# Mish as one ScalarE activation in the second feed-forward layer of a chunked attention kernel

## The chip, the cores and the metric

One NeuronCore of one Trainium2 chip. The metric is the device time of one execution in microseconds (us). Engines are named as in the profile: PE is TensorE, PEld its weight loads, DVE VectorE, ACT ScalarE, POOL GpSimd, SP SyncE, which issues the DMAs.

## What is computed

Attention within chunks of 64 tokens, then two feed-forward layers of width 512 to 2048 to 512 over 2304 tokens. The weights come as float64, the rest as float32. Of the reference, what matters:

```python
# attention per head, per chunk of 64 tokens: softmax(q k^T / sqrt(64)) v; x is its output, [2304, 512]
h = x @ moe_w_in;  r = np.maximum(h, 0.0);  g = s * (r * r) + b;  x = g @ moe_w_out      # layer one
h = x @ moe2_w_in                                                                       # layer two
sp = np.where(h > 20.0, h, np.log1p(np.exp(np.minimum(h, 20.0))))
g = h * np.tanh(sp)
out = g @ moe2_w_out
```

The last activation, h * tanh(softplus(h)), is what is called Mish.

## The kernel before

**Tiling.** Everything is held transposed on chip in `xT` (4 x 128 features by 2304 tokens). Each layer runs over five blocks of tokens; in layer one they have 512, 256, 512, 512 and 512 tokens, in layer two 512, 512, 512, 512 and 256. Per block a loop runs over 16 chunks `f` of 128 columns of d_ff. One step of it is `mm_in` (line 321: 12 matmuls into the PSUM tile `hp`), the activation (`ew1` or `ew2`) and `mm_out` of an earlier chunk (line 379: 12 matmuls into four accumulators). Each factor is split in a rounded part `hi` and a rest `lo`, and three products are taken (hi hi, lo hi, hi lo), which makes 24 matmuls of a full chunk. In the last block of layer two, with 256 tokens, a chunk has 12 matmuls of 256 columns and 6 of 512. `mm_out` comes one chunk behind `mm_in` in layer one, two behind in layer two (`LAG`), eight in the last block (`LASTLAG`).

**Activations.** `ew1` of layer one: ScalarE Relu out of PSUM (line 339), VectorE square and scale (340), ScalarE add (343), ScalarE Copy to `ghi` (344), GpSimd subtraction to `glo` (345). `ew2` of layer two computes tanh(log1p(e)) as m / (m + 2) with m = e (e + 2): VectorE minimum (355), ScalarE Exp (356), VectorE (357), ScalarE Ln (358), VectorE product with `hp` (359), ScalarE Exp (360), VectorE (362), GpSimd product (363), VectorE (364); then ScalarE Copy to `ghi` (367) and GpSimd subtraction to `glo` (368).

**Weights.** Each layer has 32 half-chunks (16 of `w_in`, 16 of `w_out`), loaded as pairs of 32-bit words (`wraw`) into room `w0_f` or `w1_f`, and made into float32 there. `decode_a`: ScalarE Abs of the upper words into the buffer `wdec` (line 105; three such buffers), VectorE clamp (106), shift (109), sign from `wraw` (113), bits of the lower words (117). `decode_b`: ScalarE Copy to `hi` (126), GpSimd subtraction to `lo` (127). Layer two's weights take the room of layer one's: in layer one's last block `w_in` of chunk f is loaded after the last use of layer one's, `w_out` one step later, and a decode comes in program order two steps after its load, at most two per step. By that, 27 of the 32 stand within layer one's last block, 5 at the start of layer two.

**Order.** The start, up to the first block, is written out by hand (`START`), the attention of the later tokens runs between steps of layer one (`at_stage`). Elsewhere the planner sets the order of instructions on each engine from a simulated timeline of its own, following program order where it can; each engine then runs its queue in that order. ScalarE's table set is chosen once ahead (line 399, `natural_log_exp_and_others`).

Of the kernel before, what the change touches and what calls it, by code (L numbers as in the profile page):

```python
# [8 lines left out]
F32 = mybir.dt.float32  # L9
F32R = mybir.dt.float32r  # L10
U32 = mybir.dt.uint32
AF = mybir.ActivationFunctionType
ALU = mybir.AluOpType
AX = mybir.AxisListType

P = 128
CH = 64
TB = 512
# [5 lines left out]
    "e2 t0 n2 t1 S3 X0 m3 T2 e3 X1 n3* A0 x0* w4 t2 T3 x1* t3 X2 A1 x2 B0 X3 w2 x3 h3 h0 h1 w5 w2 l0 l1* "  # L24
    "h2 l3* B1 l2"
)
# Upper words of float64 whose exponents are the ends of float32's range, read as float32.
UPPER_MIN = 2.0 ** -15
UPPER_MAX = (2.0 - 2.0 ** -3 - 2.0 ** -23) * 2.0 ** 16

# [2 lines left out]
def chunk_attention_moe_moe_kernel(  # L33
# [10 lines left out]
    w_out2: bass.AP,  # L44
    out: bass.AP,
):
    """The weights come as the 8-byte words of float64."""
    nc = tc.nc
    B, H, S, D = q.shape
    NT, DM = out.shape  # L50
# [4 lines left out]
    scale = 1.0 / float(D) ** 0.5  # L55
# [4 lines left out]
        1: [(sum(sizes1[:i]), n) for i, n in enumerate(sizes1)],  # L60
        2: [(sum(sizes2[:i]), n) for i, n in enumerate(sizes2)],
    }
    # 32-bit words: [..., column, (lower, upper)]
    w_dram = {
        1: (w_in1.bitcast(U32), w_out1.bitcast(U32)),
        2: (w_in2.bitcast(U32), w_out2.bitcast(U32)),
# [2 lines left out]
    sb = ctx.enter_context(tc.tile_pool(name="sb", bufs=1))  # L69
# [4 lines left out]
    ident = sb.tile([P, P], F32, name="ident")  # L74
    s_sb = sb.tile([P, 1], F32, name="s_sb")
    b_sb = sb.tile([P, 1], F32, name="b_sb")
    two = sb.tile([P, 1], F32, name="two")
    xT = sb.tile([P, KD, NT], F32, name="xT")

# [1 line left out]
    raw = {}  # L81
    wt = {}

# [16 lines left out]
    def decode_a(l, f, part):  # L100
        t = raw[l, f, part]
        a = sb.tile([P, DM], F32, tag="dec", bufs=NDEC, name="wdec")
        raw[l, f, part] = a
        u = a.bitcast(U32)
        nc.scalar.activation(out=a, in_=t[:, :, 1].bitcast(F32), func=AF.Abs)
        nc.vector.tensor_scalar(  # L106
            out=a, in0=a, scalar1=UPPER_MIN, scalar2=UPPER_MAX, op0=ALU.max, op1=ALU.min
        )
        nc.vector.tensor_scalar(  # L109
            out=u, in0=u, scalar1=3, scalar2=0x3FFFFFFF,  # L110
            op0=ALU.logical_shift_left, op1=ALU.bitwise_and,
        )
        nc.vector.scalar_tensor_tensor(  # L113
            out=u, in0=t[:, :, 1], scalar=0xC0000000, in1=u,
            op0=ALU.bitwise_and, op1=ALU.bitwise_or,
        )
        nc.vector.scalar_tensor_tensor(  # L117
            out=u, in0=t[:, :, 0], scalar=29, in1=u,
            op0=ALU.logical_shift_right, op1=ALU.bitwise_or,
        )  # L120
# [6 lines left out]
        nc.gpsimd.tensor_tensor(out=lo, in0=a, in1=hi.bitcast(F32), op=ALU.subtract)  # L127
        wt[l, f, part] = (hi, lo)

# [1 line left out]
    def runs(t0, n):  # L131
        done = 0
        while done < n:
# [2 lines left out]
            yield done, step, bb, ss  # L136
            done += step

    NS = 4  # tiles before the first block
    at = {}  # L140
    kbd = {}
    early = {}
# [10 lines left out]
        return ps_t.tile(shape, F32, tag="t", name="pt_")  # L153

    def sb_at(i, tag):
        """Tiles ahead of the first block use the room of weights that come later."""
        if i >= NS:
            if tag == "pt":  # in place of what was transposed
                return at[i]["e"].rearrange("p h s -> p (h s)")
            return atp.tile([P, DM], F32, tag=tag, name=tag)  # L160
        if (i, tag) not in early:
            pair = {"q": "w0_%d" % (15 - i), "k": "w0_%d" % (15 - i), "v": "w1_%d" % (15 - i),
                    "qt": "w1_%d" % (15 - i), "e": "w0_%d" % (11 - i), "pt": "w0_%d" % (11 - i)}
            two_t = sb.tile([P, 2, DM], F32, tag=pair[tag], name=tag)
            both = [x for x in pair if pair[x] == pair[tag]]
            for n, x in enumerate(both):
                early[i, x] = two_t[:, n]
        return early[i, tag]
# [107 lines left out]
            load_v(i + 1)  # L276

    def stages():
        """Softmax of a tile runs beside the transposes of the next one's operands."""
        yield [(NS, k_pe, k_out)]  # L280
        yield [(NS, q_pe, q_out)]
        for i in range(NS, NTILE):
            g = [(i - 1, x_pe, x_out)] if i > NS else []
            g.append((i, s_pe, s_max, s_exp, s_sum))
            if i + 1 < NTILE:
                yield g + [(i + 1, k_pe, k_out)]
                yield [(i + 1, q_pe, q_out)]
            else:
                yield g
            yield [(i, p_pe, p_out)]  # L290
        yield [(NTILE - 1, x_pe, x_out)]

# [1 line left out]
    def split_hi(t0, n, a):  # L294
        hi = sb.tile([P, TB], F32R, tag=f"xhi{a}", name=f"xhi{a}")[:, :n]
        nc.scalar.activation(out=hi, in_=xT[:, a, t0:t0 + n], func=AF.Copy)
# [28 lines left out]
        return hp  # L325

    def g_tiles(n, slot):
        if slot is not None:  # room of a weight chunk that has been used up
            t = sb.tile([P, 2, TB], F32R, tag=slot, name="g")
            return t[:, 0, :n], t[:, 1, :n]  # L330
        return (
            sb.tile([P, TB], F32R, tag="ghi", bufs=3, name="ghi")[:, :n],
            sb.tile([P, TB], F32R, tag="glo", bufs=3, name="glo")[:, :n],
        )
# [11 lines left out]
        return hi, lo  # L346

    def ew2(hp, n, slot):
        # tanh(log1p(e)) = m / (m + 2) with m = e * (e + 2)
        e = m2.tile([P, TB], F32, tag="e", bufs=2, name="me")[:, :n]  # L350
        m = m2.tile([P, TB], F32, tag="m", bufs=2, name="mm")[:, :n]
        hm = m2.tile([P, TB], F32, tag="hm", bufs=2, name="mh")[:, :n]
        r = m2.tile([P, TB], F32, tag="r", bufs=2, name="mr")[:, :n]
        hi, lo = g_tiles(n, slot)
        nc.vector.tensor_scalar(out=e, in0=hp, scalar1=20.0, scalar2=None, op0=ALU.min)
        nc.scalar.activation(out=e, in_=e, func=AF.Exp)  # L356
        nc.vector.scalar_tensor_tensor(out=m, in0=e, scalar=2.0, in1=e, op0=ALU.add, op1=ALU.mult)  # L357
        nc.scalar.activation(out=r, in_=m, func=AF.Ln, bias=two[:, 0:1])  # L358
        nc.vector.tensor_tensor(out=hm, in0=m, in1=hp, op=ALU.mult)  # L359
        nc.scalar.activation(out=r, in_=r, func=AF.Exp, scale=-1.0)  # L360
        # one Newton step on r = 1 / (m + 2)
        nc.vector.scalar_tensor_tensor(out=m, in0=m, scalar=2.0, in1=r, op0=ALU.add, op1=ALU.mult)  # L362
        nc.gpsimd.tensor_tensor(out=hm, in0=hm, in1=r, op=ALU.mult)  # L363
        nc.vector.scalar_tensor_tensor(  # L364
            out=hm, in0=m, scalar=2.0, in1=hm, op0=ALU.subtract, op1=ALU.mult, reverse0=True
        )
        nc.scalar.activation(out=hi, in_=hm, func=AF.Copy)  # L367
        nc.gpsimd.tensor_tensor(out=lo, in0=hm, in1=hi.bitcast(F32), op=ALU.subtract)  # L368
        return hi, lo

    def mm_out(l, f, g, acc, n):
# [24 lines left out]
    if True:  # L396
        atx = ExitStack()
        atp = atx.enter_context(tc.tile_pool(name="atp", bufs=1))
        nc.scalar.preload_act_table_set("natural_log_exp_and_others")
        order = sorted([(f, p) for f in range(NF) for p in range(2)], key=lambda z: (z[0] + z[1], z[1]))  # L400
        for w in LOADS.split():
            i = int(w[1:])
# [9 lines left out]
        with tc.manual_schedule():  # L412
            zero = sb.tile([P, P], F32, name="zero")
            nc.vector.memset(zero, 0.0)
            make_identity(nc, ident)
            nc.vector.memset(two, 2.0)
            warm = ps_t.tile([P, TB], F32, tag="t", name="warm")

            def warm_up(n):
# [53 lines left out]
        for si, (l, bi, f) in enumerate(steps):  # L473
            t0, n = blocks[l][bi]
            if (l, bi, f) == (2, 0, 0):
                atx.close()
                m2 = ctx.enter_context(tc.tile_pool(name="m2", bufs=1, reuse_waits="tile"))
# [3 lines left out]
            hp = mm_in(l, f, x, n)  # L481
# [50 lines left out]
```

## Time and profile before

| | us |
|---|---|
| median of 3 runs | 977.28 |
| lowest and highest | 977.11, 979.4 |
| span of the profiled execution, first to last instruction | 975.8 |

| stretch of the profiled execution | us |
|---|---|
| attention's first tiles and layer one up to its last block | 0 to about 435 |
| layer one, last block, with the decode of layer two's weights | about 435 to 550 |
| layer two, five blocks | about 550 to 972 |
| last evacuations and stores | to 975.8 |

The page gives the span alone; what an execution takes outside of it is in the times. Borders of blocks are blurred by some instructions of neighbouring blocks. Busy times overlap between engines, so they don't add up to the span; where an engine's idle time is listed, the instruction or engine that ended it stands behind the arrow.

### The profile page before, as it was taken

What the parts mean: (1) busy time and instruction counts of PE and PEld (TensorE: products, weight loads), DVE (VectorE), ACT (ScalarE), POOL (GpSimd) and SP (SyncE); (2) the same over time, 40 slices, a digit from 0 to 9 for tenths busy, and PEclk for the clock granted to TensorE, in tenths of its full rate; (3) what the DMA queues carried; (4) which work ended last, traced back from release to release, by engine and by line L of the source; (5) the groups of instructions that cost most, each with busy time, mean ns of one, the idle gap of its engine ahead of it and who ended that gap; (6) DMA issues with size and microseconds to landing.
All of it is one profiled execution on the core that took longest, in us unless ns stands there. A gap on an engine that the chain in (4) does not pass through costs nothing.

```text
span 975.8 us, 13100 instructions
## 1 busy us (share of the span) xinstructions
PE 901.6 (92%) x4880; PEld 732.4 (75%) x4880; DVE 645.9 (66%) x901; ACT 488.9 (50%) x852; POOL 437.8 (45%) x322
## 2 busy tenths in 40 slices
PE   8788779999999999999787788999999999999998
PEld 7656557998888888887565566887877787788786
DVE  5999994334222421138999998687668667866796
ACT  4655656555444533345555544454444445544553
POOL 3565553121122122225665457545554555555564
PEclk9999889999999999999899989999999999999999
DMA  8893101122211000016344100001001000100010
GB/s 186 265 346 99 33 23 44 44 55 45 47 40 33 15 9 1 1 44 193 108 151 134 60 1 1 1 6 38 1 1 44 1 1 1 44 1 0 1 45 21
DMA packets 81535, 53.27 MB, mean 55 GB/s; under 512 B 58688, under 2 KB 75072, under 8 KB 81472
## 3 DMA queue, kind: packets, MB, share of 16 engines
q1 hardware_dynamic: 81472, 52.44, 18.6%
q8 instruction: 38, 0.62, 0.3%
q14 instruction: 25, 0.20, 0.1%
HBM read 47.71 MB, written 4.72 MB: 54 GB/s over the span
## 4 chain that ended last, share of the span: by engine, by line
PE 35%; DVE 30%; ACT 10%; issue 9%; POOL 9%; SPq 3%; DMA 2%; POOLq 0%; ACTq 0%; DVEq 0%
PE acc L379 16%; PE hp L321 15%; POOL mh L363 7%; DVE wdec L113 5%; DVE mm L357 4%; DVE mh L364 4%; DVE wdec L117 4%; DVE wdec L106 4%; ACT ghi L367 3%; ACT mr L358 2%; DVE wdec L109 2%; ACT mr L360 2%; DVE mm L362 2%; DVE r L340 2%; DVE xlo L301 1%
## 5 line engine op out<-in xcount | busy, mean ns | idle before, releaser
L321 PE MATMUL hp<-xhi,w 128*128 128x512 f32 (+1 forms) x1280 | 377.0, 374 | 20.2 <-DVE mh L359 7.8
L321 PEld LDWEIGHTS hp<-xhi,w 128*128 128x128 f32 x1280 | 233.1, 190 | 66.9 <-DVE mh L359 10.1
L321 PE MATMUL hp<-xlo,w 128*128 128x512 f32 (+1 forms) x640 | 237.1, 372 | 4.2 <-DVE xlo L301 4.0
L345 POOL TENSOR_TENSOR glo<-r,ghi 128x512 fp32r<-128x512 f32 (+1 forms) x80 | 104.9, 1312 | 246.2 <-ACT ghi L344 202.8
L379 PE MATMUL acc<-ghi,w 128*128 128x512 f32 (+1 forms) x640 | 158.4, 388 | 16.1 <-ACT ghi L344 15.0
L340 DVE SCALAR_TENSOR_TENSOR r<-r,s_sb 128x512 f32<-128x512 f32 (+1 forms) x80 | 63.9, 800 | 164.3 <-ACT r L339 164.1
L363 POOL TENSOR_TENSOR mh<-mh,mr 128x512 f32<-128x512 f32 (+1 forms) x80 | 123.6, 1547 | 79.9 <-ACT mr L360 62.2
L379 PEld LDWEIGHTS acc<-ghi,w 128*128 128x128 f32 x640 | 114.4, 195 | 43.3 <-ACT ghi L344 19.2
L379 PE MATMUL acc<-w,ghi 128*128 128x512 f32 x516 | 134.6, 400 | 11.9 <-ACT ghi L367 11.2
L321 PEld LDWEIGHTS hp<-xlo,w 128*128 128x128 f32 x640 | 121.4, 190 | 26.7 <-DVE xlo L301 6.5
L127 POOL TENSOR_TENSOR w<-wdec,w 128x512 fp32r<-128x512 f32 x64 | 96.3, 1511 | 87.8 <-ACT w L126 83.6
L368 POOL TENSOR_TENSOR glo<-mh,ghi 128x512 fp32r<-128x512 f32 (+1 forms) x65 | 88.6, 1366 | 93.2 <-ACT ghi L367 93.2
L379 PEld LDWEIGHTS acc<-w,ghi 128*128 128x128 f32 x516 | 95.5, 190 | 41.6 <-ACT ghi L367 21.7
L367 ACT ACTIVATE ghi<-mh 128x512 fp32r<-128x512 f32 (+1 forms) x65 | 40.8, 628 | 96.7 <-DVE mh L364 96.6
L357 DVE SCALAR_TENSOR_TENSOR mm<-me 128x512 f32<-128x512 f32 (+1 forms) x80 | 76.5, 958 | 18.6 <-ACT me L356 18.4
L358 ACT ACTIVATE mr<-mm,two 128x512 f32<-128x512 f32 (+1 forms) x80 | 54.3, 681 | 68.2 <-DVE mm L357 67.9
L379 PE MATMUL acc<-glo,w 128*128 128x512 f32 (+1 forms) x320 | 83.4, 381 | 3.8 <-POOL glo L345 3.8
L364 DVE SCALAR_TENSOR_TENSOR mh<-mm,mh 128x512 f32<-128x512 f32 (+1 forms) x80 | 58.8, 737 | 41.9 <-POOL mh L363 41.6
L339 ACT ACTIVATE r<-hp 128x512 f32<-128x512 f32 (+1 forms) x80 | 43.8, 548 | 82.3 <-PE hp L321 81.2
L362 DVE SCALAR_TENSOR_TENSOR mm<-mm,mr 128x512 f32<-128x512 f32 (+1 forms) x80 | 59.1, 740 | 37.6 <-ACT mr L360 36.9
L126 ACT ACTIVATE w<-wdec 128x512 fp32r<-128x512 f32 x64 | 40.3, 630 | 79.1 <-DVE wdec L117 79.1
L343 ACT ACTIVATE r<-r,b_sb 128x512 f32<-128x512 f32 (+1 forms) x80 | 54.4, 680 | 38.8 <-DVE r L340 38.7
(301 smaller groups left out, 1101.9 us busy)
## 6 DMA issues: line engine op xcount, KB each, us to landing
wraw<-in_moe_w_out_dram SPq DMA_DIRECT2D x32, 512.0 KB, 4.4
wraw<-in_moe_w_in_dram SPq DMA_DIRECT2D x32, 512.0 KB, 4.8
v<-in_v_dram SPq DMA_DIRECT2D x72, 64.0 KB, 2.8
out_dram<-o SPq DMA_DIRECT2D x18, 256.0 KB, 2.2
k<-in_k_dram SPq DMA_DIRECT2D x16, 256.0 KB, 3.1
q<-in_q_dram SPq DMA_DIRECT2D x12, 256.0 KB, 3.0
k<-in_q_dram SPq DMA_DIRECT2D x4, 256.0 KB, 4.7
k<-in_k_dram SPq DMA_DIRECT2D x4, 128.0 KB, 5.8
```

What stands on the lines that cost most here:

```text
L127: nc.gpsimd.tensor_tensor(out=lo, in0=a, in1=hi.bitcast(F32), op=ALU.subtract)
L321: nc.tensor.matmul(out=hp, lhsT=w[:, sl], rhs=r, start=(a == 0 and p == 0), stop=(a == KD - 1 and p == 2),)
L340: nc.vector.scalar_tensor_tensor(out=r, in0=r, scalar=s_sb[:, 0:1], in1=r, op0=ALU.mult, op1=ALU.mult)
L345: nc.gpsimd.tensor_tensor(out=lo, in0=r, in1=hi.bitcast(F32), op=ALU.subtract)
L357: nc.vector.scalar_tensor_tensor(out=m, in0=e, scalar=2.0, in1=e, op0=ALU.add, op1=ALU.mult)
L358: nc.scalar.activation(out=r, in_=m, func=AF.Ln, bias=two[:, 0:1])
L362: nc.vector.scalar_tensor_tensor(out=m, in0=m, scalar=2.0, in1=r, op0=ALU.add, op1=ALU.mult)
L363: nc.gpsimd.tensor_tensor(out=hm, in0=hm, in1=r, op=ALU.mult)
L364: nc.vector.scalar_tensor_tensor(out=hm, in0=m, scalar=2.0, in1=hm, op0=ALU.subtract, op1=ALU.mult, reverse0=True)
L367: nc.scalar.activation(out=hi, in_=hm, func=AF.Copy)
L368: nc.gpsimd.tensor_tensor(out=lo, in0=hm, in1=hi.bitcast(F32), op=ALU.subtract)
L379: nc.tensor.matmul(out=acc[m][:, :n] if l == 1 else acc[m], lhsT=w[wi][:, sl] if l == 1 else g[gi][:, sl], rhs=g[gi] if l == 1 else w[wi], ...
```

## The change

`ew2` becomes three instructions: one ScalarE activation Mish out of PSUM into `r` (three buffers in place of two), the Copy to `ghi` and the subtraction to `glo`. In `decode_a` the Abs of layer two's weights (`l == 2`) becomes an and with 0x7FFFFFFF on VectorE; layer one's stay on ScalarE. The table set chosen ahead is `exp_and_others`, and the constant `two` goes.

```diff
-        nc.scalar.activation(out=a, in_=t[:, :, 1].bitcast(F32), func=AF.Abs)
+        if l == 1:
+            nc.scalar.activation(out=a, in_=t[:, :, 1].bitcast(F32), func=AF.Abs)
+        else:
+            nc.vector.tensor_scalar(
+                out=u, in0=t[:, :, 1], scalar1=0x7FFFFFFF, scalar2=None, op0=ALU.bitwise_and
+            )
...
     def ew2(hp, n, slot):
-        # tanh(log1p(e)) = m / (m + 2) with m = e * (e + 2)
-        e = m2.tile([P, TB], F32, tag="e", bufs=2, name="me")[:, :n]
-        m = m2.tile([P, TB], F32, tag="m", bufs=2, name="mm")[:, :n]
-        hm = m2.tile([P, TB], F32, tag="hm", bufs=2, name="mh")[:, :n]
-        r = m2.tile([P, TB], F32, tag="r", bufs=2, name="mr")[:, :n]
+
+        r = m2.tile([P, TB], F32, tag="r", bufs=3, name="mr")[:, :n]
         hi, lo = g_tiles(n, slot)
-        nc.vector.tensor_scalar(out=e, in0=hp, scalar1=20.0, scalar2=None, op0=ALU.min)
-        nc.scalar.activation(out=e, in_=e, func=AF.Exp)
-        nc.vector.scalar_tensor_tensor(out=m, in0=e, scalar=2.0, in1=e, op0=ALU.add, op1=ALU.mult)
-        nc.scalar.activation(out=r, in_=m, func=AF.Ln, bias=two[:, 0:1])
-        nc.vector.tensor_tensor(out=hm, in0=m, in1=hp, op=ALU.mult)
-        nc.scalar.activation(out=r, in_=r, func=AF.Exp, scale=-1.0)
-        # one Newton step on r = 1 / (m + 2)
-        nc.vector.scalar_tensor_tensor(out=m, in0=m, scalar=2.0, in1=r, op0=ALU.add, op1=ALU.mult)
-        nc.gpsimd.tensor_tensor(out=hm, in0=hm, in1=r, op=ALU.mult)
-        nc.vector.scalar_tensor_tensor(
-            out=hm, in0=m, scalar=2.0, in1=hm, op0=ALU.subtract, op1=ALU.mult, reverse0=True
-        )
-        nc.scalar.activation(out=hi, in_=hm, func=AF.Copy)
-        nc.gpsimd.tensor_tensor(out=lo, in0=hm, in1=hi.bitcast(F32), op=ALU.subtract)
+        nc.scalar.activation(out=r, in_=hp, func=AF.Mish)
+        nc.scalar.activation(out=hi, in_=r, func=AF.Copy)
+        nc.gpsimd.tensor_tensor(out=lo, in0=r, in1=hi.bitcast(F32), op=ALU.subtract)
         return hi, lo
...
-        nc.scalar.preload_act_table_set("natural_log_exp_and_others")
+        nc.scalar.preload_act_table_set("exp_and_others")
```

## Rows read from the trace of the kernel before

**Rows 1.** The page, part 1: span; busy time and share of TensorE and VectorE.
```profile
span 975.8 us, 13100 instructions
PE 901.6 (92%) x4880; PEld 732.4 (75%) x4880; DVE 645.9 (66%) x901; ACT 488.9 (50%) x852; POOL 437.8 (45%) x322
```

**Rows 2.** Table by stages: stretch, its length, busy us and count of each engine.
```profile
core 0: us, PE busy (x) PEld busy (x) DVE busy (x) ACT busy (x) POOL busy (x), PEclk, DMA share, GB/s
...
434.60:549.60 115.00, 95.62 (x389) 72.95 (x388) 107.68 (x132) 61.83 (x106) 66.43 (x41) 0.97 0.43 137
549.60:606.00 56.40, 45.31 (x179) 34.75 (x178) 52.94 (x64) 28.26 (x46) 35.53 (x23) 0.94 0.04 10
606.00:657.00 51.00, 51.00 (x227) 42.25 (x226) 36.92 (x48) 23.99 (x39) 24.62 (x17) 1.00 0.00 0
657.00:749.00 92.00, 89.57 (x387) 71.68 (x386) 65.47 (x86) 43.22 (x70) 48.94 (x32) 1.00 0.03 12
749.00:842.00 93.00, 90.30 (x389) 71.58 (x388) 66.47 (x88) 44.25 (x72) 48.91 (x32) 1.00 0.03 12
842.00:917.20 75.20, 72.64 (x313) 57.77 (x312) 51.59 (x70) 36.16 (x60) 42.18 (x28) 1.00 0.04 15
917.20:971.70 54.50, 52.16 (x313) 45.39 (x311) 44.68 (x92) 28.57 (x72) 30.86 (x36) 1.00 0.05 20
```

**Rows 3.** Timeline of TensorE: start us, length us, engine, line, what, count.
```profile
944.39 1.55 PE L379 MATMUL acc<-w,g 128*128 128x512 f32 x6
945.77 0.40 PE L321 MATMUL hp<-xhi,w 128*128 128x256 f32 x2
946.01 0.28 PE L321 MATMUL hp<-xlo,w 128*128 128x256 f32 x1
```

**Rows 4.** The same stretch table for lines 321 and 379 alone, last block.
```profile
917.20:971.70 54.50, 25.50 (x192) 24.39 (x191) 1.00 0.05 20
...
917.20:971.70 54.50, 30.05 (x121) 21.65 (x120) 1.00 0.05 20
```

**Rows 5.** Waits of TensorE, 438 to 550, then 550 to 610: us, times, longest.
```profile
PE acc L379 <- ACT ghi L344: 8.9, 7, 3.7
...
PE hp L321 <- DVE mh L359: 6.8, 3, 2.8
```

**Rows 6.** The page, part 5: groups by line, count, busy, mean, idle before.
```profile
L368 POOL TENSOR_TENSOR glo<-mh,ghi 128x512 fp32r<-128x512 f32 (+1 forms) x65 | 88.6, 1366 | 93.2 <-ACT ghi L367 93.2
L367 ACT ACTIVATE ghi<-mh 128x512 fp32r<-128x512 f32 (+1 forms) x65 | 40.8, 628 | 96.7 <-DVE mh L364 96.6
L339 ACT ACTIVATE r<-hp 128x512 f32<-128x512 f32 (+1 forms) x80 | 43.8, 548 | 82.3 <-PE hp L321 81.2
```

**Rows 7.** Groups by line, ScalarE: the table load.
```profile
L399 ACT ACT_TABLE_LOAD x1 | 1.3, 1283 | 0.7 <-PEq L516 0.7
```

**Rows 8.** Groups by line, VectorE, 438 to 550.
```profile
L106 DVE TENSOR_SCALAR wdec<-wdec 128x512 f32<-128x512 f32 x28 | 21.4, 766 | 5.1 <-ACT wdec L105 5.1
L109 DVE TENSOR_SCALAR wdec<-wdec 128x512 uint32<-128x512 uint32 x27 | 18.7, 694 | 0.3
```

**Rows 9.** Line 106 (ns: min/median/max), then the timeline of VectorE.
```profile
L106 DVE TENSOR_SCALAR wdec<-wdec x64: 407/416/1526, 23.5 to 564.3; 128x512 f32<-128x512 f32 x64
...
459.04 0.42 DVE L106 TENSOR_SCALAR wdec<-wdec 128x512 f32<-128x512 f32 x1
459.38 0.68 DVE L113 SCALAR_TENSOR_TENSOR wdec<-wraw,wdec 128x512 uint32<-128x512 uint32 x1
459.98 0.42 DVE L109 TENSOR_SCALAR wdec<-wdec 128x512 uint32<-128x512 uint32 x1
...
465.15 1.26 DVE L106 TENSOR_SCALAR wdec<-wdec 128x512 f32<-128x512 f32 x1 [0.19 <-ACT wdec L105]
```

**Rows 10.** Timeline of GpSimd in the same stretch.
```profile
462.69 4.86 POOL L127 TENSOR_TENSOR w<-wdec,w 128x512 fp32r<-128x512 f32 x3
```

## What the change does to the time

> **What bounds the kernel now.** I read the page's first part first: TensorE is busy for 92% of the 975.8 us, VectorE for 66% [rows 1]. A busy TensorE can still be a slow one, so the second view is the table by stages, where the count of matmuls in a stretch can be set against its length [rows 2]. The price of a matmul that nothing holds up comes from a timeline of TensorE late in the kernel: six matmuls of 512 columns start at 944.39 and the next instruction at 945.77, so 0.23 us each; two of 256 columns take from 945.77 to 946.01, so 0.12 us each [rows 3]. Over longer runs it is slightly less: 227 in the 51.0 us from 606 to 657 are 0.225 us each, and I use 0.227 and 0.12 [rows 2, 3].
>
> Count times price, against the length of the stretch [rows 2]:
> - 434.6 to 549.6, the last block of layer one: 389 x 0.227 = 88.3 of 115.0 us; 26.7 lost.
> - 549.6 to 606, the start of layer two: 179 x 0.227 = 40.6 of 56.4 us; 15.8 lost.
> - 606 to 657: 227 x 0.227 = 51.5 of 51.0 us; nothing lost.
> - 657 to 749, 749 to 842, 842 to 917.2: 387, 389 and 313 matmuls make 87.8, 88.3 and 71.1 us of 92.0, 93.0 and 75.2; 4.2, 4.7 and 4.1 lost.
> - 917.2 to 971.7, mostly the last block of 256 tokens: 192 x 0.12 + 121 x 0.227 = 50.5 of 54.5 us [rows 4]; 4.0 lost.
>
> So layer two loses 15.8 + 4.2 + 4.7 + 4.1 + 4.0 = 32.8 us beyond its matmuls, and the last block of layer one 26.7. The change can give back the first sum; the second belongs to the decode, which it makes longer on VectorE. In that block VectorE is busy for 107.7 of 115.0 us [rows 2], and the longest waits of TensorE there are for ScalarE's `ghi` of line 344, which stands at the end of a chain that passes VectorE's line 340. From 550 to 610 the longest is for VectorE's line 359, a link of the ten-step chain [rows 5].
>
> **Part 1, the chain of layer two.** Per chunk of d_ff the change removes five VectorE instructions (lines 355, 357, 359, 362, 364), three ScalarE activations (356, 358, 360) and one GpSimd multiply (363), and adds one activation out of PSUM; the Copy of line 367 and the GpSimd subtraction of line 368 stay. The nearest row for Mish is line 339, an activation from PSUM to the same shape: 548 ns. The new chain is then 0.55 (Mish) + 0.63 (Copy) + 1.37 (subtraction), about 2.6 us plus hand-overs [rows 6]. The output matmuls of a chunk come two chunks behind its input matmuls, which is 2 x 24 x 0.227 = 10.9 us of TensorE work, so this chain is covered four times over. Layer one, with a chain of the same kind and a lag of one chunk only, is what such a stage looks like when nothing else presses; the stretch from 606 shows that even the old chain reaches the cadence at times. ScalarE has 1.2 us of such work per 5.4 us chunk, so it doesn't become the bound, and GpSimd has one instruction in place of two. The PSUM tile `hp` is free after one activation in place of being held up to line 359. I give back all of layer two's loss but 5 us: up to 4 at its start, where five decodes are left over and TensorE's first output matmuls wait for the first `ghi`, and 1 at the end. Gain: 32.8 - 5 = 28 us. Bounds: 24 us if the start keeps half of its 15.8 and the blocks lose 1 more, 33 if nothing is left.
>
> The end itself isn't changed: after the last matmul come the same evacuation and the same two stores. ScalarE's table is loaded once now, 1.28 us at the start [rows 7]; the new kernel needs a second load ahead of its first Mish. It lies in ScalarE's queue in front of work that has 10.9 us of lag, so I cost it at nothing; without that cover it is 1.3 us, once. The memset of `two` is one small VectorE instruction that falls away; nothing.
>
> The Trainium skill ("ScalarE: Activation LUTs", What ACT_TABLE_LOAD costs) puts a switch of sets at about 2.66 us, the drain with it, and says that the function doesn't change an activation's price. The trace has a load of 1.28 us and no switch; by the page the sum would be 1.4 us more at most, if uncovered.
>
> **Part 2, the sign on VectorE.** For each of the 32 half-chunks of layer two's weights, ScalarE's Abs (line 105) becomes a VectorE and-mask on words that lie 8 bytes apart. By the code, 27 of the 32 decodes stand in the last block of layer one and 5 in the first of layer two (line 109 shows 27 in that stretch [rows 8]). There VectorE has no room: 7.3 us of 115.0 idle, of which 5.1 are waits of line 106 for the very Abs that goes [rows 2, 8]. What does one more instruction cost?
>
> The trace doesn't show this operation with this operand. The nearest rows are lines 109 and 106, the same kind with one operand, packed: 694 and 766 ns as means of the stretch [rows 8]. These means mix two lengths. Line 106 runs from 407 to 1526 ns with a median of 416 [rows 9]. In the timeline it takes 0.42 us with its successor starting 0.34 us later; while GpSimd works through three `w` subtractions from 462.69 to 467.55, line 106 takes 1.26 us [rows 9, 10]. The long form is the short one with a wait for GpSimd in it, about 1.1 us, and it comes with GpSimd's instructions, whose number in this block doesn't change. One more VectorE instruction should thus add its own length and not one more wait. I take 0.34 us, from the start-to-start of the free form: 27 x 0.34 = 9.2 us. Against that, the waits for Abs: the mask needs only the landed words and a free buffer, and ScalarE no longer stands between them; I take 3 of the 5.1 us back, since some of them are waits for the buffer that GpSimd frees. The last block of layer one grows by 9.2 - 3 = 6 us. Bounds: from 5.1 us shorter (the mask lies in idle time, all waits go) to 27 x 0.766 = 20.7 us longer (each mask at the mean of line 106, no wait recovered). If the 8-byte step costs the quick form, the free length is that of line 113 in the timeline, which reads the same words: 0.60 us to the next start [rows 9], 16.2 us in all, inside the bounds. The five others meet a VectorE that has nothing else to do.
>
> "SBUF — State Buffer" of the Trainium skill (SBUF: two separate sides) says why the long form exists: VectorE and GpSimd take a shared pair of ports as a lock, for a whole instruction. By that rule the mask costs its own length whether GpSimd is there or not, which is the forecast; the trace's two lengths agree with it. The Trainium skill's "ScalarE: Activation LUTs" also has abs in every table set (Table sets: the hidden batching unit). By that the sign could have stayed on ScalarE, and the 6 us would not be spent; no row here has Abs beside Mish.
>
> **The sum.** 975.8 - 28 + 6 = 953.8 us of span. The page gives the profiled execution's span alone; the median of the three runs is 977.28, 1.5 us above it, for what lies outside the first and last instruction. Forecast: 953.8 + 1.5 = 955.3, I say 955 us.
>
> **The rivals.**
> - A, the mask at full price: 27 x 0.766 = 20.7 us and nothing recovered, as VectorE is the bound there. 975.8 - 28 + 20.7 + 1.5 = 970 us. For it: nearly every idle spell of VectorE in that block is already gone; against it: the number of GpSimd's instructions, with which the long forms come, stays. 0.20.
> - B, the mask hides: the block shortens by 5.1 and layer two loses nothing. 975.8 - 33 - 5.1 + 1.5 = 939 us. For it: ScalarE's queue no longer has Abs waiting for a buffer in front of line 344; against it: VectorE at 94%. 0.10.
> - C, slower: each mask brings a wait for GpSimd of its own, so that its price is the long form, 1.5 us [rows 9], in the one block where VectorE sets the pace: 27 x 1.5 = 40.5 us. 975.8 - 28 + 40.5 + 1.5 = 990 us. It decides from 28 / 27 = 1.04 us per mask on; the means of 0.69 and 0.77 us for its two neighbours speak against it. 0.06.
> - D, the change doesn't stay one load: if Mish and Copy don't share a table, every chunk has two loads. ScalarE then needs 1.2 + 2 x 1.28 = 3.8 us per full chunk, under the 5.4 of TensorE, but in the 16 half chunks of the last block, at the full chunk's price as an upper end, 3.8 us against 12 x 0.12 + 6 x 0.227 = 2.8 us: 16 x 1.0 = 16 us at most. 955 + 16 = 971 us. 0.04.
>
> **How the numbers follow.** The forecast, with what lies around it (947 to 963), has 0.60, A 0.20, B 0.10, C 0.06, D 0.04. The range of 942 to 971 us takes in the forecast, A, D and most of what lies towards B; it leaves out C, the last of B, and a little beyond A. About 0.3%, 2.9 us, is what a measurement of this kernel can tell from no change. Faster by more than that (below 974.3) are the forecast, B, D and nearly all of A: 0.89; within it, the far side of A: 0.05; slower, C: 0.06.
>
> **What would show it.** Right: from the start of layer two, matmuls at 0.227 us with hardly a wait, VectorE nearly idle there, one more table load; and the last block of layer one some 121 us long, with 27 masks of either 0.4 or 1.5 us, the long ones no more numerous than GpSimd's instructions. Wrong, if that block takes over 135 us or under 112; if TensorE in layer two still waits for `ghi`; or if the order of work set by the planner, which sees other durations than before, moves decodes across the border of the two layers.

## The result and the profile after

The changed kernel takes 955.26 us (median of 4 runs, 954.56 to 956.55), the kernel before 978.34 us beside it (4 runs); the ratio is 0.976, 95% interval 0.9745 to 0.9776. The forecast was 955 us, range 942 to 971. The profiled execution's span is 953.1 us, 22.7 us shorter than before.

Part 1 of the page after, to set beside [rows 1]: the span, and the busy time of each engine.

```profile
span 953.1 us, 12183 instructions
PE 889.1 (93%) x4880; PEld 731.7 (77%) x4880; DVE 368.9 (39%) x532; ACT 378.1 (40%) x661; POOL 309.7 (32%) x242
```

VectorE's busy time has fallen from 645.9 to 368.9 us, and TensorE's share has hardly moved, from 92 to 93%: the share alone would have told little. The stages do. This is the table of stages after, with the columns of [rows 2]: stretch, its length, busy us and count of PE, PEld, DVE, ACT and POOL, granted clock, DMA share and GB/s. The first row is the last block of layer one, the second the start of layer two.

```profile
434.10:555.00 120.90, 96.90 (x386) 72.45 (x385) 113.46 (x159) 47.72 (x81) 65.89 (x41) 0.97 0.41 131
555.00:572.00 17.00, 12.53 (x49) 9.87 (x48) 16.69 (x22) 5.96 (x11) 10.88 (x8) 0.90 0.10 32
572.00:657.00 85.00, 85.00 (x377) 70.38 (x375) 6.41 (x8) 23.98 (x41) 23.36 (x18) 1.00 0.03 13
657.00:749.00 92.00, 92.00 (x407) 76.20 (x406) 4.12 (x6) 24.18 (x40) 21.97 (x17) 1.00 0.03 12
749.00:842.00 93.00, 93.00 (x412) 76.99 (x411) 4.12 (x6) 24.61 (x41) 21.99 (x17) 1.00 0.03 12
842.00:895.00 53.00, 53.00 (x236) 43.88 (x234) 0.46 (x2) 12.88 (x22) 12.93 (x10) 1.00 0.00 1
895.00:949.00 54.00, 54.00 (x329) 48.35 (x327) 2.63 (x5) 16.27 (x39) 13.08 (x17) 1.00 0.05 20
```

Count times 0.227 us, as in the prediction: 386 x 0.227 = 87.6 of 120.9 us, 33.3 lost; 49 x 0.227 = 11.1 of 17.0, 5.9 lost. From 572 on nothing is lost that this count can show: 377, 407, 412 and 236 matmuls make 85.6, 92.4, 93.5 and 53.6 us in 85.0, 92.0, 93.0 and 53.0 (a matmul that straddles a border counts on both sides). In the last row 197 matmuls are of 256 columns and 132 of 512: 23.6 + 30.0 = 53.6 of 54.0 us. VectorE is busy for about 4 us of 92 there, against 65 to 66 before [rows 2].

| stretch | lost before, us | lost after, us |
|---|---|---|
| last block of layer one | 26.7 | 33.3 |
| layer two | 32.8 | 6.3 |
| both | 59.5 | 39.6 |

That is 19.9 us of the span's 22.7; half a us lies in an earlier start of the block (434.1 against 434.6), the rest in the rounding of the counts at the borders. The two borders are alike: the last matmul of layer one ends at 549.6 before and at 555.0 after. By the timelines both kernels have lost the same 40 us at layer two's 144th matmul, which stands at 589.0 and 588.3 us. Up to there the masks take what the shorter chain gives; the gain in the span lies behind that point.

What TensorE still waits for between 430 and 620, after (total us, times, longest):

```profile
PE acc L369 <- ACT ghi L348: 12.1, 8, 2.7
PE acc L369 <- POOL glo L349: 5.2, 5, 1.5
PE hp L325 <- ACT r L343: 5.0, 4, 2.0
PE acc L369 <- ACT xT L380: 4.5, 1, 4.5
PE hp L325 <- DVE xlo L305: 1.6, 2, 1.1
```

These waits make 28.4 of the 39.2 us lost in the first two stretches. A part of the rest is TensorE's clock, which the count of losses takes in. After the change the granted clock is at 0.50, the lower of its two levels (1.2 GHz), in three pieces of 3.4 us, from 482.4, 523.3 and 564.3. Each comes within 1.2 us of the end of one of TensorE's long waits (2.7, 2.0 and 4.5 us). These pieces hold 27 matmuls, which at 0.227 us make 6.1 of the 10.2 us, so about 4 us are lost in them. Before, there are two pieces of 6.8 us, from 479.9 and 561.8, with 26 matmuls, 5.9 of 13.6 us, and waits among them. So of the 19.9 us up to 3.6, an estimate from these counts, lie in stretches at the lower clock, where the cost of the clock and that of the waits weren't told apart.

The waits of [rows 5] for VectorE's link of the old chain are gone; those for `ghi` of layer one (line 348 now, 344 before) have grown from 8.9 to 12.1 us. The groups of VectorE from 438 to 560, by line (count, busy us, mean ns, idle before), then line 107, the mask, over the whole run (ns: min/median/max):

```profile
L110 DVE TENSOR_SCALAR wdec<-wdec 128x512 f32<-128x512 f32 x28 | 19.8, 714 | 0.1
L107 DVE TENSOR_SCALAR wdec<-wraw 128x512 uint32<-128x512 uint32 x29 | 17.3, 600 | 6.0 <-POOL w L131 6.0
L113 DVE TENSOR_SCALAR wdec<-wdec 128x512 uint32<-128x512 uint32 x28 | 16.7, 602 | 0.2
...
L107 DVE TENSOR_SCALAR wdec<-wraw x32: 409/415/1519, 433.3 to 567.4; 128x512 uint32<-128x512 uint32 x32
```

The mask has the two lengths of line 106 before [rows 9], 0.41 and about 1.5 us. It waits for GpSimd's release of a buffer, as ScalarE's Abs did before, from 438 to 550 (us, times, longest):

```profile
ACT wdec L105 <- POOL w L127: 7.4, 5, 2.8
```

### The profile page after: what moved, and what is told of

The parts are those of the page before. It is cut to its first block, busy times and chain, and to the rows that moved or that the text cites. A ratio compares the mean times of both kernels' runs of the same rounds, so it can differ in the third digit from the quotient of the medians.

```text
span 953.1 us, 12183 instructions
## 1 busy us (share of the span) xinstructions
PE 889.1 (93%) x4880; PEld 731.7 (77%) x4880; DVE 368.9 (39%) x532; ACT 378.1 (40%) x661; POOL 309.7 (32%) x242
## 4 chain that ended last, share of the span: by engine, by line
PE 69%; DVE 19%; issue 5%; SPq 2%; DMA 2%; ACT 1%; POOL 1%; POOLq 0%; DVEq 0%; ACTq 0%
PE acc L369 33%; PE hp L325 32%; DVE wdec L117 5%; DVE wdec L110 3%; DVE wdec L121 3%; DVE wdec L113 2%; DMA wraw<-in_moe_w_in_dram 2%; DVE r L344 2%; DVE wdec L107 2%; SPq L190 1%; POOL w L131 1%; SPq L177 1%; DVE xlo L305 1%; SPq L92 0%; ACT w L130 0%
## 5 line engine op out<-in xcount | busy, mean ns | idle before, releaser
L325 PE MATMUL hp<-xhi,w 128*128 128x512 f32 (+1 forms) x1280 | 371.6, 373 | 12.0 <-ACT r L343 5.0
L358 POOL TENSOR_TENSOR glo<-mr,ghi 128x512 fp32r<-128x512 f32 (+1 forms) x65 | 84.2, 1296 | 246.1 <-ACT ghi L357 246.1
L369 PEld LDWEIGHTS acc<-ghi,w 128*128 128x128 f32 x640 | 112.4, 192 | 49.8 <-ACT ghi L348 26.7
L356 ACT ACTIVATE mr<-hp 128x512 f32<-128x512 f32 (+1 forms) x80 | 44.2, 553 | 249.8 <-PE hp L325 249.8
L305 DVE TENSOR_TENSOR xlo<-xT,xhi 128x512 fp32r<-128x512 f32 (+1 forms) x38 | 28.2, 755 | 280.6 <-PE hp L325 204.2
L344 DVE SCALAR_TENSOR_TENSOR r<-r,s_sb 128x512 f32<-128x512 f32 (+1 forms) x80 | 61.5, 769 | 164.4 <-ACT r L343 164.2
L369 PEld LDWEIGHTS acc<-w,ghi 128*128 128x128 f32 x516 | 97.6, 190 | 25.1 <-ACT xT L380 4.9
L369 PE MATMUL acc<-w,glo 128*128 128x512 f32 x258 | 72.5, 390 | 0.0
L369 PEld LDWEIGHTS acc<-glo,w 128*128 128x128 f32 x320 | 57.5, 192 | 19.0 <-POOL glo L349 8.8
L117 DVE SCALAR_TENSOR_TENSOR wdec<-wraw,wdec 128x512 uint32<-128x512 uint32 x64 | 64.6, 1012 | 0.5
L121 DVE SCALAR_TENSOR_TENSOR wdec<-wraw,wdec 128x512 uint32<-128x512 uint32 x64 | 63.1, 988 | 0.4
```

What stands on the lines that cost most here:

```text
L117: nc.vector.scalar_tensor_tensor(out=u, in0=t[:, :, 1], scalar=0xC0000000, in1=u, op0=ALU.bitwise_and, op1=ALU.bitwise_or,)
L121: nc.vector.scalar_tensor_tensor(out=u, in0=t[:, :, 0], scalar=29, in1=u, op0=ALU.logical_shift_right, op1=ALU.bitwise_or,)
L325: nc.tensor.matmul(out=hp, lhsT=w[:, sl], rhs=r, start=(a == 0 and p == 0), stop=(a == KD - 1 and p == 2),)
L344: nc.vector.scalar_tensor_tensor(out=r, in0=r, scalar=s_sb[:, 0:1], in1=r, op0=ALU.mult, op1=ALU.mult)
L356: nc.scalar.activation(out=r, in_=hp, func=AF.Mish)
L358: nc.gpsimd.tensor_tensor(out=lo, in0=r, in1=hi.bitcast(F32), op=ALU.subtract)
```

## The experiments

All times are medians in us; each stands beside the kernel before as it was measured with it. "Lost" is a stretch's length less its matmuls at 0.227 us.

| kernel | us | kernel before | ratio, 95% interval |
|---|---|---|---|
| the change | 955.3 | 978.3 | 0.9745 to 0.9776 |
| Mish, Abs kept on ScalarE | 948.9 | 979.9 | 0.9672 to 0.9701 |
| old chain, mask on VectorE | 986.0 | 979.9 | 1.0043 to 1.0073 |
| mask twice | 955.1 | 979.9 | 0.9724 to 0.9756 |
| Abs in layer one, mask in layer two | 949.4 | 979.9 | 0.9669 to 0.9698 |
| five idle VectorE instructions | 956.9 | 977.9 | 0.9757 to 0.9800 |
| chain longer on ScalarE | 955.8 | 977.9 | 0.9747 to 0.9783 |
| slower decode | 956.4 | 977.9 | 0.9751 to 0.9793 |
| slower decode, Abs in layer one | 953.3 | 977.9 | 0.9724 to 0.9773 |
| old chain, lag of three | 982.7 | 978.2 | 1.0030 to 1.0060 |
| square on ScalarE | 949.6 | 978.2 | 0.9689 to 0.9718 |
| the same, Abs in layer one | 947.0 | 978.2 | 0.9662 to 0.9695 |
| square on ScalarE, Copy on VectorE | 957.4 | 979.1 | 0.9762 to 0.9795 |

The kernel before itself stands between 977.9 and 979.9 us in this table. A difference between two kernels that stand beside different times of it is therefore sure to about 2 us only.

### One part of the change at a time

Mish alone, with Abs left where it was:

```diff
-        if l == 1:
-            nc.scalar.activation(out=a, in_=t[:, :, 1].bitcast(F32), func=AF.Abs)
-        else:
-            nc.vector.tensor_scalar(out=u, in0=t[:, :, 1], scalar1=0x7FFFFFFF, ...)
+        nc.scalar.activation(out=a, in_=t[:, :, 1].bitcast(F32), func=AF.Abs)
```

> Mish in layer two, but Abs stays on ScalarE for all decodes. Theory (the mask costs the last block of layer one about 6 us): that block takes 115 us as before, layer two about 394 as after, 949 us in all; at most ten more table loads of 1.28 us at the start of layer two, where five Abs stand among the first Mish, and they are covered. Rival 1 (the mask hides in waits that Abs makes): 955 us. Rival 2 (each Abs beside Mish costs two uncovered loads): 949 + 5 x 2.6 = 962 us.

Measured: 948.9 us, as the theory has it, and 6.4 under the whole change (7.3 by the two ratios). The table loads of this kernel (groups by line on ScalarE: line 351 is its Mish, 104 its Abs, 384 the load chosen ahead):

```profile
L351 ACT ACT_TABLE_LOAD x3 | 3.8, 1283 | 0.1
L104 ACT ACT_TABLE_LOAD x2 | 2.6, 1283 | 0.0
L384 ACT ACT_TABLE_LOAD x1 | 1.3, 1283 | 0.7 <-PEq L500 0.7
```

Three loads stand ahead of a Mish and two ahead of an Abs, so as this kernel is built, the set that serves Mish doesn't serve Abs. The Trainium skill ("ScalarE: Activation LUTs", Table sets: the hidden batching unit) lists abs among the functions of every set; this run shows otherwise. The next run but one shows what the loads cost.

The old chain with the mask alone (the same lines, put into the kernel before):

> The ten-step chain of before, only the sign moved to VectorE for layer two's weights. Theory: the 27 masks lengthen the last block of layer one by 6 us and the five others add 5 x 0.34 = 1.7 at the start of layer two, where VectorE is full with the old chain: 978 + 8 = 986 us. Rival A (each at 0.77 us, nothing recovered): 978 + 25 = 1003 us. Rival B (hidden): 978 us or less.

Measured: 986.0 us, 6.1 over the kernel before; the theory has 8, rival A 25, rival B nothing. Both single parts thus give the price of the mask as about 6 us, once added and once taken away.

Abs for the decodes that are issued during layer one, the mask for the last five:

```diff
-        if l == 1:
+        if not mask:
             nc.scalar.activation(out=a, in_=t[:, :, 1].bitcast(F32), func=AF.Abs)
...
-                    decode_w(2, *decodes.pop(0)[1:])
+                    decode_w(2, *decodes.pop(0)[1:], mask=l == 2)
```

> Mish in layer two; the 27 decodes issued during layer one take their sign off with Abs on ScalarE, the five issued in layer two with the mask on VectorE. Theory: the last block of layer one is back at 115 us, no table load but one: 949 us. Set beside the run with Abs everywhere it tells what the loads cost: equal if they are covered. Rival (the mask cost nothing): 955 us.

Measured: 949.4 us, equal to the run with Abs everywhere within 0.5 us. The four more table loads of that run, 1.28 us each, are covered: they cost nothing that can be seen.

### What a mask costs

> The changed kernel with each mask of layer two's decode issued twice in a row. Theory (a mask costs its own 0.34 us and brings no wait for GpSimd of its own): 27 x 0.34 = 9 us more in the last block of layer one, 964 us. Rival A (0.77 us each): 976 us. Rival C (1.5 us each): 996 us. Rival B (hidden): 955 us.

The edit repeats the and-mask on the same operands. Measured: 955.1 us, which is rival B's number for the second mask, against 6 us for the first. The decode sequence itself tells why this isn't a free instruction. The last instruction of a decode, by line on VectorE, in the stretch from the first decode to the end of the 24th: before, 434 to 532.2;

```profile
L117 DVE SCALAR_TENSOR_TENSOR wdec<-wraw,wdec 128x512 uint32<-128x512 uint32 x24 | 22.3, 929 | 0.3
```

with Abs in layer one (its line 121 is the same instruction), also 434 to 532.2;

```profile
L121 DVE SCALAR_TENSOR_TENSOR wdec<-wraw,wdec 128x512 uint32<-128x512 uint32 x24 | 22.3, 930 | 0.3
```

after, 433 to 539.3;

```profile
L121 DVE SCALAR_TENSOR_TENSOR wdec<-wraw,wdec 128x512 uint32<-128x512 uint32 x24 | 22.5, 944 | 0.1
```

and with the mask twice (lines 107 and 110), 433 to 552.2:

```profile
L124 DVE SCALAR_TENSOR_TENSOR wdec<-wraw,wdec 128x512 uint32<-128x512 uint32 x24 | 18.4, 771 | 0.0
L107 DVE TENSOR_SCALAR wdec<-wraw 128x512 uint32<-128x512 uint32 x26 | 17.5, 675 | 10.7 <-POOL w L134 8.3 <-DMA wraw<-in_moe_w_in_dram 2.4
```

By the timelines the first of these decodes begins at 434.7, 434.6, 433.3 and 433.5 us and the 24th ends at 532.0, 532.1, 539.2 and 552.1. So 24 decodes take 97.3, 97.5, 105.9 and 118.6 us: the first mask adds 8.6 / 24 = 0.36 us to a decode, the second 12.7 / 24 = 0.53. The first is close to the 0.34 us of the forecast (over 28 decodes it is 9.3 us, 0.33 each). The second lengthens the decodes too, but not the kernel. From the first matmul of layer one's last block to its last, TensorE loses 33.6 us after and 35.7 with two masks; from there to layer two's 144th matmul it loses 6.2 and 4.1, so both have lost 39.8 us at that point. With Abs in layer one it is 34.5. The border between the layers is where the two orders differ. ScalarE, then TensorE, in the timeline after:

```profile
563.29 0.63 ACT L130 ACTIVATE w<-wdec 128x512 fp32r<-128x512 f32 x1 [2.98 <-DVE wdec L121]
563.83 1.05 ACT L380 COPY xT<-acc 128x512 f32<-128x512 f32 x2
...
564.45 2.08 PE L369 MATMUL acc<-w,ghi 128*128 128x512 f32 x4 [4.47 <-ACT xT L380]
```

The two evacuations of layer one's last accumulators (line 380) stand in ScalarE's queue behind the Copy of a decode (line 130), which has waited 2.98 us for VectorE; TensorE's first output matmul of layer two waits 4.47 us for them. With two masks the wait at this place is 2.3 us, for VectorE's evacuation. The mask doesn't make this wait: it is 2.9 us with Abs in layer one and 3.2 with Abs everywhere. How much of a longer decode reaches the end thus hangs in part on what the planner's order puts at the border; that this alone hides the second mask is not shown. That another order would have made the first mask free too wasn't tried.

### Load or length: what layer two lost

Five VectorE instructions of the old chain's sizes, beside the chain:

```diff
         nc.scalar.activation(out=r, in_=hp, func=AF.Mish)
...
+        nc.vector.tensor_scalar(out=z, in0=hp, scalar1=20.0, scalar2=None, op0=ALU.min)
+        nc.vector.scalar_tensor_tensor(out=y, in0=z, scalar=2.0, in1=z, op0=ALU.add, op1=ALU.mult)
+        nc.vector.tensor_tensor(out=y, in0=y, in1=hp, op=ALU.mult)
+        nc.vector.scalar_tensor_tensor(out=z, in0=y, scalar=2.0, in1=z, op0=ALU.add, op1=ALU.mult)
+        nc.vector.scalar_tensor_tensor(out=z, in0=z, scalar=2.0, in1=y, op0=ALU.subtract, op1=ALU.mult)
```

> The changed kernel with five VectorE instructions per chunk of layer two put back, in the sizes of the old chain's, beside the chain: nothing waits for their result, but they read hp and so hold its PSUM tile. Theory 1 (layer two lost its time to VectorE's load): the start of layer two loses about 10 us again, the later blocks little: 965 us. Theory 2 (it lost it to the length of the chain through three engines): 955 us. Theory 3 (load throughout): 978 us or more.

Four more Copies in the chain:

```diff
         nc.scalar.activation(out=r, in_=hp, func=AF.Mish)
+        for _ in range(4):
+            nc.scalar.activation(out=r, in_=r, func=AF.Copy)
```

> The changed kernel with four more ScalarE Copies in each chunk's chain between Mish and ghi, 4 x 0.6 = 2.4 us, so that the chain takes about 5 us and ScalarE 3.6 of 5.4 us per chunk. Theory 1 (10.9 us of lag cover the chain): 955 us, and at most 3 us more at the start of layer two. Theory 2 (length decides): some of the 4 us per block come back, 965 to 971 us.

Measured: 956.9 and 955.8 us, neither more than 1.6 us above the change. The stretch from 600 to 900, with the columns of the stages, first with the idle VectorE instructions,

```profile
600.00:900.00 300.00, 300.00 (x1327) 248.55 (x1327) 228.03 (x307) 79.62 (x132) 94.14 (x56) 1.00 0.03 11
```

then with the longer chain:

```profile
600.00:900.00 300.00, 300.00 (x1328) 248.59 (x1328) 16.55 (x22) 216.79 (x354) 71.01 (x55) 1.00 0.03 11
```

VectorE is busy for 76% of that stretch in the first, more than the 71% of the old chain's steady blocks (65.47 of 92 us [rows 2]), and ScalarE for 72% in the second, and yet 1327 and 1328 matmuls at 0.227 us fill the 300 us. So neither the load of VectorE alone nor a chain of about 5 us alone costs layer two anything there. (GpSimd's load is not put back in the first: 31% against 53% in the old chain's steady blocks, so the load of both engines together stays untested.) What is left is a chain that stands in the queue of the loaded engine, and its whole length against its cover. ScalarE's longest wait before, from 610 to 972 (us, times, longest), is of that kind:

```profile
ACT ghi L367 <- DVE mh L364: 86.0, 53, 2.7
```

The timelines hold the chain's length as well, from a chunk's last input matmul to the end of its `ghi`. Over 50 chunks, the 13th to the 62nd of layer two, it takes 7.6 to 15.1 us before, with a median of 11.7. The cover of two chunks is 10.9. So the old chain overran its cover in 41 of the 50. After the change it takes 1.4 us, with the idle VectorE instructions 1.4, with the four Copies 4.0. More cover for the old chain (and one buffer more of `ghi` and of `glo`):

```diff
-        LAG = {1: 1, 2: 2}
+        LAG = {1: 1, 2: 3}
```

> The kernel before, with the output matmuls of layer two three chunks behind in place of two (16.3 us of cover for the ten-step chain in place of 10.9) and one more ghi and glo buffer. Theory (in its steady blocks layer two lost 4 to 6 us each because the old chain, through a busy VectorE, at times overran its cover): these losses shrink from 19 to under 5 us, 978 - 14 = 964 us; the start of layer two is not mended. Rival (VectorE and GpSimd together set the pace, so more cover only moves the wait): 975 us or more.

Measured: 982.7 us, slower than before by 0.3 to 0.6%. The theory's 964 us didn't come; the time is the rival's case (975 or more): the wait moved. The waits of TensorE's weight loads in layer two, which come ahead of its matmuls, show where to. Before, 610 to 972 (us, times, longest):

```profile
PEld acc L379 <- ACT ghi L367: 16.2, 24, 1.7
```

With a lag of three, 600 to 980:

```profile
PEld hp L321 <- ACT xhi L296: 11.3, 5, 3.6
PEld hp L321 <- DVE xlo L301: 4.5, 5, 1.2
PEld acc L379 <- DVE o L393: 3.4, 3, 1.4
PEld acc L379 <- ACT ghi L367: 1.5, 3, 0.6
```

The waits for `ghi`, 16.2 us beside the 17.0 lost from 606 on, have gone down to 1.5, as the theory has it: the chain takes 13.0 us in the median now, but has 16.3 of cover. But the split of the next block's input (`xhi`, `xlo`) and the evacuations of `o` now come late at the borders of the blocks, 11.3 + 4.5 + 3.4 us of waits which take the place of those removed. Why they come late wasn't followed further.

### What is left in the last block of layer one

> The changed kernel with one decode per step, and two in every fourth, in place of up to two: 1.25 per step, so that about ten of the 32 move from the last block of layer one into the first of layer two, where VectorE is idle now. Theory (VectorE and GpSimd in turn set the pace of that block): a step then needs 1.25 x 2.22 + 0.66 + 2.25 x 1.1 = 5.9 us of both beside TensorE's 5.4, so the block loses about 7 us in place of 33, and the first block of layer two needs 1.25 x 2.22 + 2.25 x 1.1 = 5.3 us a step and loses little: 955 - 26 = 929 us. Rival (weights come late in layer two, or the planner undoes it): 950 us or more.

```diff
-            for _ in range(2):
+            for _ in range(2 if si % 4 == 0 else 1):
```

Measured: 956.4 us; the rival's case (950 or more). The planner put the decodes back: their last instruction has the same count as after in the same stretch, here 433 to 539.4.

```profile
L121 DVE SCALAR_TENSOR_TENSOR wdec<-wraw,wdec 128x512 uint32<-128x512 uint32 x24 | 22.5, 943 | 0.1
```

> Both: the slower decode, with Abs on ScalarE for the decodes issued during layer one and the mask for those in layer two. Theory: the step of the last block needs 1.25 x 1.88 + 0.66 + 2.25 x 1.1 = 5.5 us of VectorE and GpSimd, near TensorE's 5.4: 923 to 929 us. Rival (nothing left to gain from Abs once the decode is slower): equal to the run with the slower decode alone.

Measured: 953.3 us, neither the theory's 923 to 929 nor the rival's 956. The order being what it was, the slower decode only changed which decodes are issued during layer two, and so carry the mask: 15 in this kernel, against 5 in the one with Abs in layer one and 32 after. The times 949.4, 953.3 and 955.3 us go the same way as these counts, and so do the losses up to layer two's 144th matmul: 34.5, 37.8 and 39.8 us.

The same cure as the change's, for layer one's activation: off VectorE.

```diff
-        nc.vector.scalar_tensor_tensor(
-            out=r, in0=r, scalar=s_sb[:, 0:1], in1=r, op0=ALU.mult, op1=ALU.mult
-        )
-        nc.scalar.activation(out=r, in_=r, func=AF.Identity, bias=b_sb[:, 0:1])
+        nc.scalar.activation(out=r, in_=r, func=AF.Square)
+        nc.scalar.activation(out=r, in_=r, func=AF.Identity, bias=b_sb[:, 0:1], scale=s_sb[:, 0:1])
```

> The changed kernel, and in layer one's activation the square on ScalarE too (Square, then the scale s within the activation that adds b), so that no activation passes VectorE any more, in either layer. Theory (in the last block of layer one TensorE waits because its chain stands in VectorE's queue among the decodes, as the chain of layer two did): the 31 us lost there and the 8 at the start of layer two fall to about 10, decodes then finish during layer two's first block: 955 - 29 = 926 us, some us less if the first block of layer one gains as well. Rival (ScalarE's queue, in which the Copy of a decode waits for VectorE, holds the chain as much): 945 us or more.

> The same with Abs on ScalarE for the decodes issued during layer one and the mask for those of layer two. Theory: the decode sequence is 27 x 0.35 = 9 us shorter, but no longer in TensorE's way: equal to the run with the mask, 926 us, within 3. Rival (the decode still sets the pace): 6 us less than that run.

Measured: 949.6 and 947.0 us. The first is 5.7 us under the change where 29 were expected; the two lie within 3 us of each other, as the second theory has it, but both over 20 us above its 926. TensorE's longest wait there from 425 to 600, and ScalarE's from 425 to 560, with the square on ScalarE and the mask on VectorE:

```profile
PE acc L367 <- ACT ghi L346: 14.3, 9, 2.1
...
ACT w L130 <- DVE wdec L121: 60.7, 25, 4.5
```

TensorE waits for `ghi` no less than after the change, 14.3 us against 12.1. ScalarE no longer waits for VectorE in the activation, but its queue also holds the Copy of each decode, which waits for VectorE 25 times, 60.7 us in all. That is the rival as written down. The second, with Abs in layer one, is 2.7 us faster than the first and the fastest kernel here, 0.9% under the change.

The last run takes that Copy out of ScalarE's queue too:

```diff
-        nc.scalar.activation(out=hi, in_=a, func=AF.Copy)
+        if l == 1:
+            nc.scalar.activation(out=hi, in_=a, func=AF.Copy)
+        else:
+            nc.vector.tensor_copy(out=hi, in_=a)
```

> The kernel with the square on ScalarE, and the Copy to hi in the decode of layer two's weights moved to VectorE, so that nothing in ScalarE's queue waits for VectorE in the last block of layer one. Theory (TensorE's waits for ghi, 14 us, and for the last evacuation, 4 us, come from activations that stand in ScalarE's queue behind a Copy which waits for VectorE): these waits go, the decode sequence becomes 32 x 0.35 = 11 us longer, mostly beside other work: 935 us. Rival (the same wait appears in GpSimd's queue, where glo stands behind a decode's subtraction): 945 to 955 us.

Measured: 957.4 us, 7.8 slower than the kernel that it starts from and past the rival's 945 to 955, though the wait is the one that the rival names. TensorE's longest wait (425 to 600), ScalarE's and GpSimd's (425 to 560):

```profile
PE acc L370 <- POOL glo L350: 18.8, 8, 3.2
...
ACT r L346 <- PE hp L328: 64.2, 13, 7.2
...
POOL w L134 <- DVE w L133: 41.1, 17, 5.4
```

ScalarE now waits only for TensorE, and the waits for `ghi` are gone. In their place stand 18.8 us for `glo`, whose subtraction stands in GpSimd's queue behind a decode's subtraction that waits for VectorE. With the decodes issued this early, each engine that these runs left with a link of both the decode and the activations, ScalarE and then GpSimd, passed VectorE's backlog on to TensorE. An order that holds the decodes back wasn't reached: the one edit that aimed at it was undone by the planner.

## Why the prediction was right, point by point

- **What bounds what.** Setting counts of matmuls against the length of a stretch gave 32.8 us that layer two could give back and 26.7 that it couldn't. After the change 6.3 us of the first are left, where 5 were forecast, nearly all at the start as foreseen.
- **The chain.** The reading that the short chain is covered held: nothing is lost from 572 on, and with four more Copies in it still nothing from 600 to 900. "Covered four times over" stands for the chain alone, which takes 2.8 us to the end of `glo` in the timeline, with 10.9 of cover; at the border the evacuation on ScalarE, which the prediction didn't look at, was not covered.
- **The reason for layer two's loss** was given as a chain through busy engines. The runs bear it out and narrow it: load beside the chain costs nothing, the old chain's median of 11.7 us is more than its 10.9 of cover, and its waits for `ghi` go with more cover. What the kernel then loses at the borders of blocks shows that a longer lag alone wouldn't have mended it. The prediction gave the whole loss to the chain and the decode; a part of it lay in stretches at a lower clock, of which it says nothing.
- **The mask.** 0.34 us each was read from the free form, and 0.36 is what 24 decodes show. That an added instruction brings no wait for GpSimd of its own held as well: between the first decode and the last, the timelines have 46 VectorE instructions over 1.15 us before and 42 after, with 51 and 49 on GpSimd. The prediction also reads this from the lock on the ports, but a lock alone has the later instruction wait; it is GpSimd's count, which hardly changed, that carries the argument. The masks themselves ran long at times (600 ns as a mean); the waits moved to them from others: line 113 has a mean of 602 ns where line 109 had 694 [rows 8]. Rivals A and C fell with this, and the quick form holds for words 8 bytes apart (median 415 ns).
- **The 3 us taken back** was a mis-sized term. Line 107 waits 6.0 us for GpSimd's release of a buffer between 438 and 560, where line 106 waited 5.1 us for Abs from 438 to 550 [rows 8]. Abs had been waiting for the same buffer, 7.4 us, and the wait went over to the mask whole, though within the first 24 decodes it was still 3.5 us against 5.1. The last block still lost only 6.6 us more than before, and the single-part runs give 6, because not all of the 9.2 us of masks reach the end. Two errors of about 3 us met here: nothing was taken back, and the masks cost less at the end than their length. That the forecast agrees to the microsecond is luck to that extent.
- **The table load** was costed at nothing, and with up to six loads in a run nothing more was seen. The 1.4 us given for an uncovered switch were too few beside a sum that has it at nothing: by the price that the prediction names it is the whole 2.66. Rival D fell: there is one load at the first Mish and none at the Copies behind it.
- **Rival B** (the mask hides) was wrong for the change, which the runs without the mask show by 6 us, but right for a second mask.

## What to carry to other kernels

An activation's chain that hops through the queue of a loaded engine is worth taking off it even where that engine's average load looks harmless; count what each stage loses against its matmuls, for the gain can't exceed that. An instruction moved onto the engine that sets a stage's pace lengthens that engine's work by about its own length, of which more or less reaches the end: keep it on the engine with room for as long as the needed function is in the table that is loaded (here Abs during layer one), and load the other table where the work changes. In-order queues pass a backlog on: before moving a link, list every instruction behind it on each engine that serves both pieces of work, evacuations among them.

## What the runs showed of the hardware

The switch of tables took 1.28 us. ScalarE's timeline after, at its only switch:

```profile
552.27 0.63 ACT L130 ACTIVATE w<-wdec 128x512 fp32r<-128x512 f32 x1 [1.58 <-DVE wdec L121]
552.92 1.28 ACT L356 ACT_TABLE_LOAD   x1
554.21 0.60 ACT L356 ACTIVATE mr<-hp 128x512 f32<-128x512 f32 x1
```

The load begins 0.02 us after the Copy before it ends and the Mish follows it at once: 1.28 us in all. The Trainium skill ("ScalarE: Activation LUTs", What ACT_TABLE_LOAD costs) gives about 2.66 us for a switch, a drain of 1.38 among them; no such drain shows here. A Mish out of PSUM takes 553 ns as a mean of both sizes, beside 549 for the Relu of line 343, which agrees with that page's statement that the function doesn't change the price. VectorE's cast of 128x512 from float32 to the rounded type, in the last run, took 0.415 us as a mean of 32, the quick form throughout.
